# Attention and two feed-forward layers on one core: when the turns of p run, on which half of the array's rows, and in how many parts their results are used

## The chip, the cores and the metric

The kernel runs on one core of a Trainium2 chip. The metric is the device time of one execution in microseconds (us), median of several runs; lower is better. PE is TensorE (matmuls and transposes; PEld its weight loads), DVE is VectorE, ACT ScalarE, POOL GpSimd, SP SyncE, which issues DMAs. All data is float32.

## The reference

Four batches of eight heads of attention over 576 positions of 64 numbers, with rotary embedding of q and k, and behind it two feed-forward layers (512 to 2048 to 512) on all 2304 rows. Only the attention is touched by the change.

```
q_rot, k_rot = rotate(q), rotate(k)
scores = scale * q_rot @ k_rot^T                       # 576 x 576 for each head
scores = scores - max(scores, axis=-1)
attn = exp(scores)
attn = attn / (sum(attn, axis=-1) + 1e-09)
x = attn @ v                                           # then rows (B*S, H*D)
g = h - tanh(h), h = x @ w_in;      x = g @ w_out      # layer 1
g = h * sigmoid(h), h = x @ w_in;   x = g @ w_out      # layer 2
```

## The kernel before

**Tiling.** Two heads make a pair; there are 16 pairs (`NP`), handled one after the other. Head 0 of a pair lies on partitions 0 to 63, head 1 on 64 to 127, so a matmul for one head uses one half of the array's rows ("half 0", "half 1"), and the two halves can work at the same time. The 576 query rows of a head are four tiles of 128 and one remainder of 64. A pair takes five cycles, z0 to z4, which the `while` loop at the end of `attention` writes out one after the other. In z0 to z3 a cycle has two score tiles, first that of head 0 (half 0), then that of head 1 (half 1), each of two matmuls of 288 columns (e = 0, 1), each of these with two passes in the trace. In z4 the two remainders of 64 rows share one tile.

**The way of one tile.** PE computes the scores into one of two buffers in PSUM (tag `sc`; `bufs=2`), DVE takes the row maximum (L514), ACT the exponential with the row sum (L526), which frees the buffer. The result p then has to be turned: `p_turn` transposes it in blocks of 64 columns (L580), eight for each half and tile, into two PSUM tiles, whence ACT or DVE copies it to SBUF (`evac`, L554 and L556; `ON_DVE` says which copies DVE makes). After that `pv` multiplies it with v (L617), into one PSUM tile with `Q0` = 256 query columns (e = 0) or the other 320 (e = 1). The division is done last: the row sums' reciprocals (DVE L531, L532) are spread by POOL (L534) and by PE transposes (`spread`, L542), copied by ACT (L546, L549), and multiplied in by DVE (L626).

**Order.** Every engine runs its instructions in the order in which the loop writes them. In a cycle of the kernel before PE is given: the scores of both tiles; the turns of p of the cycle before (`pu`: lag one), alternating between the halves; the `full_block` (spread, remainder, the last turns, each on the whole array); and four, four, six, four or two products with v of the pair before (`PV_N`; e = 1 in z1 and z2, e = 0 in z3, z4 and the next z0). ACT first makes the two exponentials, then the copies.

**The next pair's work.** POOL applies the rotary embedding to the next pair's k and q (`rope_ops`, three operations for each of five parts: 0 and 1 are q, 2 and 3 are k, 4 the remainder of both, tiles `ar` and `br`). `rope_push` queues them in the order (2, 3, 0, 1, 4) and four are taken in each cycle. PE turns the result for one half in eight transposes (`qk_turn`, L434) in the cycles that `QK_AT` names. The conversion of the feed-forward weights (`conv`, L133 to L166) is spread over the cycles on DVE, ACT, POOL and SP.

**Start and end.** For pair 0 nothing lies ahead, and `warm` puts idle transposes in PE's way (L484). After pair 15 a few cycles finish the products with v, together with the first feed-forward work.

Of the kernel before, what the change touches and what calls it, by code (L numbers as in the profile page):

```python
# [29 lines left out]
def kernel(  # L30
# [298 lines left out]
    WARM_Z = (0, 7, 7, 5, 3, 5)  # L329
    ON_DVE = ((1, 1), (2, 1), (4, 1))  # L330
    QK_AT = ((4, 3), (4, 1), (4, 0))
# [4 lines left out]
    def attention(conv, on_rope_done, on_scores_near, on_scores_done):  # L336
# [90 lines left out]
        def qk_turn(i, w):  # L427
# [71 lines left out]
        def scores(g):  # L499
            i, n = divmod(g, NTI)  # L500
            h, j = tiles[n]
            kq = qk_t[i]
            sc = score_tile(g)
            for e in range(2):
                for w in ((h,) if h < 2 else (0, 1)):
                    r = half[w]
                    o, c, n = (slice(0, 128), REM + j * 128, 128) if h < 2 else (r, 0, REM)
                    k0 = (0 if h == 1 else REM) + e * HALF
                    PE.matmul(sc[o, e, 0:HALF], lhsT=kq[r, 1, c:c + n], rhs=kq[r, 0, k0:k0 + HALF],  # L509
                              start=True, stop=True)  # L510
# [18 lines left out]
        def recips(i):  # L529
            r = ap.tile([128, 2, NTI], F32, tag="rr", name="rr", bufs=2)  # L530
            DVE.tensor_scalar(out=r[:, 0], in0=sum_t.pop(i), scalar1=1e-9, scalar2=None, op0=ALU.add)  # L531
            DVE.reciprocal(out=r[:, 1], in_=r[:, 0])  # L532
            wide = ap.tile([128, NTI + 1, 64], F32, tag="rw", name="rw", bufs=2)
            POOL.tensor_copy(out=wide[:, 0:NTI], in_=r[:, 1].unsqueeze(2).to_broadcast([128, NTI, 64]))  # L534
            POOL.tensor_copy(out=wide[:, NTI:], in_=r[:, 1, NTI - 1:].unsqueeze(2).to_broadcast([128, 1, 64]))
            r_t[i] = wide.rearrange("p n d -> p (n d)")

        def spread(i, e, tp):
            r = r_t[i] if e else r_t.pop(i)
            for j in ((2, 3, 4) if e else (0, 1)):  # L540
                o = j * 128 - e * Q0
# [134 lines left out]
        while True:  # L676
# [13 lines left out]
            for g in gs:  # L690
                scores(g)
# [574 lines left out]
```

## Time and profile before

| | |
|---|---|
| time, median of 3 runs | 1085.2 us (1084.88 to 1085.38) |
| the profiled execution | 1085.18 us, its span on the core 1083.4 us |
| PE busy | 1071.4 us (99%) |
| DVE, ACT, POOL busy | 817.6, 650.1, 240.1 us |
| pairs 0 and 1 | 8.95 to 43.68 us |
| pairs 2 to 14 | 43.68 to 265.12 us, 17.03 us for each |
| pair 15 and the tail | 265.12 to about 298.5 us |
| feed-forward layers | to 1083.4 us |

PE is busy for almost the whole span, and in the pairs 2 to 14 for all of it; both halves of its rows count as one PE there. A row of the timeline joins instructions of one kind that follow or overlap each other: its second number is the time from the first one's start to the last one's end, and "x8" how many there are.

### The profile page before, as it was taken

How to read it: one execution, taken by the hardware profiler on the slowest of the kernel's cores; microseconds unless marked ns; L12 is line 12 of the kernel's file. 1: busy time of each engine (PE TensorE's matmuls, PEld its weight loads, DVE VectorE, ACT ScalarE, POOL GpSimd, SP SyncE). 2: the span in 40 equal slices, each digit the busy share in tenths (PEclk: the TensorE clock that was granted, in tenths of full speed). 3: DMA queues.
4: the chain of work that ended last, by engine and by line, in shares of the span. 5: the costliest groups of instructions: out<-in, count | busy, mean ns of one | idle time of the engine just before them, and what ended most of it. 6: DMA issues, size and time to landing. Idle time of an engine off the chain costs nothing.

```text
span 1083.4 us, 19054 instructions
## 1 busy us (share of the span) xinstructions
PE 1071.4 (99%) x7026; PEld 874.3 (81%) x7026; DVE 817.6 (75%) x1407; ACT 650.1 (60%) x1411; POOL 240.1 (22%) x311
## 2 busy tenths in 40 slices
PE   9999999999999999999999999999999999999998
PEld 7677767777688898888778898888888889999997
DVE  6677777777588968999999979986556357767775
ACT  5788788887777667768656657434433335334342
POOL 6878686772011100212010100310000000000000
PEclk9999999999999999999999999999999999999999
DMA  5243333322314324533745532565434213122042
GB/s 174 72 112 87 115 94 105 112 83 71 106 45 146 117 78 125 172 112 124 223 140 196 194 98 79 192 202 188 138 117 154 88 40 99 67 68 88 29 138 78
DMA packets 91277, 126.35 MB, mean 117 GB/s; under 512 B 16432, under 2 KB 57008, under 8 KB 91184
## 3 DMA queue, kind: packets, MB, share of 16 engines
q1 hardware_dynamic: 90592, 124.75, 36.4%
q8 instruction: 55, 0.90, 0.4%
q10 hardware_dynamic: 592, 0.39, 0.1%
q14 instruction: 38, 0.31, 0.1%
HBM read 88.93 MB, written 36.18 MB: 115 GB/s over the span
## 4 chain that ended last, share of the span: by engine, by line
PE 94%; issue 2%; POOL 2%; ACT 1%; DMA 1%; DVE 0%; SPq 0%; POOLq 0%; DVEq 0%
PE hp L829 35%; PE acc L906 26%; PE sc L509 9%; PE x L617 8%; PE M L990 7%; PE tpp L580 4%; PE tpq L434 1%; PE acc L1134 1%; PE tpb L542 1%; PE tpb L596 1%; DMA wf<-wd 0%; POOL bm L416 0%; ACT p L526 0%; DMA xm<-in_k_dram 0%; POOL w L251 0%
## 5 line engine op out<-in xcount | busy, mean ns | idle before, releaser
L829 PE MATMUL hp<-xh,w 128*128 128x512 f32 (+1 forms) x1280 | 388.1, 369 | 0.0
L829 PEld LDWEIGHTS hp<-xh,w 128*128 128x128 f32 x1280 | 234.5, 189 | 41.8 <-issue 1.6
L829 PE MATMUL hp<-xl,w 128*128 128x512 f32 (+1 forms) x640 | 235.9, 369 | 0.0
L840 ACT ACTIVATE t<-hp 128x512 f32<-128x512 f32 (+1 forms) x120 | 66.8, 557 | 247.3 <-PE hp L829 247.3
L906 PE MATMUL acc<-gh,w 128*128 128x512 f32 (+1 forms) x640 | 195.2, 371 | 4.0 <-ACT w L250 3.4
L874 DVE TENSOR_TENSOR gl<-t,gh 128x512 fp32r<-128x512 f32 (+1 forms) x120 | 77.5, 645 | 109.5 <-ACT gh L872 109.1
L514 DVE TENSOR_REDUCE st<-sc 128x1 f32<-128x576 f32 x144 | 103.4, 754 | 68.5 <-PE sc L509 67.3
L906 PEld LDWEIGHTS acc<-gh,w 128*128 128x128 f32 x640 | 117.8, 190 | 25.3 <-ACT w L250 3.8
L829 PEld LDWEIGHTS hp<-xl,w 128*128 128x128 f32 x640 | 120.7, 189 | 19.3
L526 ACT ACTIVATE p<-sc,st 128x576 f32<-128x576 f32 x144 | 105.4, 736 | 32.0 <-DVE st L514 32.0
L251 POOL TENSOR_TENSOR w<-wf,w 128x512 fp32r<-128x512 f32 x32 | 45.4, 1431 | 355.8 <-ACT w L250 352.3
L906 PE MATMUL acc<-gl,w 128*128 128x512 f32 (+1 forms) x320 | 118.3, 370 | 0.0
L509 PE MATMUL sc<-kq 64*128 64x288 f32 (+1 forms) x640 | 115.0, 426 | 0.8 <-ACT p L526 0.6
L509 PEld LDWEIGHTS sc<-kq 64*128 64x128 f32 (+1 forms) x640 | 68.9, 175 | 41.3 <-ACT p L526 16.1
L906 PE MATMUL acc<-w,gh 128*128 128x512 f32 x288 | 88.9, 390 | 0.0
L617 PE MATMUL x<-pt,vm 128*64 128x256 f32 (+1 forms) x512 | 79.1, 421 | 0.0
L872 ACT ACTIVATE gh<-t 128x512 fp32r<-128x512 f32 (+1 forms) x120 | 70.6, 588 | 6.2 <-PE acc L906 6.2
L990 PE MATMUL M<-w,gh 128*128 128x256 f32 x384 | 70.3, 283 | 0.0
L906 PEld LDWEIGHTS acc<-gl,w 128*128 128x128 f32 x320 | 60.8, 190 | 10.1
L580 PE MATMUL tpp<-ident,p 64*128 64x64 f32 x1248 | 68.2, 225 | 0.0
L580 PEld LDWEIGHTS tpp<-ident,p 64*128 64x128 f32 x1248 | 63.5, 138 | 4.0 <-DVE xl L811 0.4
L990 PEld LDWEIGHTS M<-w,gh 128*128 128x128 f32 x384 | 61.8, 191 | 2.3
(135 smaller groups left out, 1878.0 us busy)
## 6 DMA issues: line engine op xcount, KB each, us to landing
raw<-in_moe_w_in_dram SPq DMA_DIRECT2D x32, 512.0 KB, 4.1
raw<-in_moe_w_out_dram SPq DMA_DIRECT2D x28, 512.0 KB, 3.7
xin<-xd SPq DMA_DIRECT2D x56, 256.0 KB, 4.5
wd<-wa SPq DMA_DIRECT2D x48, 256.0 KB, 2.2
wf<-wd SPq DMA_DIRECT2D x48, 256.0 KB, 3.9
pd<-xo SPq DMA_DIRECT2D x34, 256.0 KB, 3.4
xo<-pd SPq DMA_DIRECT2D x18, 256.0 KB, 5.6
xm<-in_q_dram SPq DMA_DIRECT2D x16, 256.0 KB, 3.2
```

The source lines that it names most:

```text
L251: (DVE if key[0] == 3 else POOL).tensor_tensor(out=w[:, 1].rearrange("p (a b) -> p a b", a=a), in0=src, in1=w[:, 0].bitcast(F32).rearrange ...
L509: PE.matmul(sc[o, e, 0:HALF], lhsT=kq[r, 1, c:c + n], rhs=kq[r, 0, k0:k0 + HALF], start=True, stop=True)
L514: DVE.tensor_reduce(out=st, in_=s_t[g][:, :, 0:HALF], op=ALU.max, axis=AX.XY, negate=True)
L526: ACT.activation(out=p.rearrange("p (e s) -> p e s", e=2), in_=sc[:, :, 0:HALF], func=ACTF.Exp, bias=st, accum_out=sum_t[i][:, n:n + 1])
L580: PE.transpose(tp[w][:, x * 64:x * 64 + 64], t[r, c:c + 128], ident[r, r])
L617: PE.matmul(x[o, 0:w], lhsT=l, rhs=r, start=(cc == 0), stop=(cc == NJ))
L829: PE.matmul(hp, lhsT=w[:, a, ws], rhs=bb, start=(n == 0), stop=(n == 3 * KD - 1))
L840: ACT.activation(out=t, in_=hp, func=ACTF.Tanh, scale=0.5 if l else 1.0)
L872: ACT.activation(out=gh, in_=t, func=ACTF.Copy)
L874: DVE.tensor_tensor(out=gl, in0=t, in1=gh.bitcast(F32), op=ALU.subtract)
L906: PE.matmul(acc, lhsT=a, rhs=bb, start=(fi == 0 and n == 0), stop=(fi == NH - 1 and n == 2))
L990: PE.matmul(prod_t[name][:, tt], lhsT=al[i], rhs=bw[j], start=(first and tt == 0 and x == 0), stop=(last and tt == nt - 1 and x == 2))
```

## The change

Five things. (1) The turns of p lag two cycles instead of one: those of tile u come two cycles after its scores (z2 turns tile 0, ..., the next pair's z0 tile 3 and z1 tile 4). (2) PE is given, in z0 to z3: the first score matmul of head 0; all turns of half 1; the other three score matmuls; all turns of half 0. So half 1 turns while half 0 does its scores, and the other way round. (3) The copies of the turned p that ACT makes come ahead of its exponentials, and DVE makes five of them in each pair instead of three. (4) Reciprocals are taken and spread in two parts: the first four row sums in z2, the other five in the next pair's z0; the products with v start with e = 0, in z4, and e = 1 takes z2 and z3. So z1 has four products of 256 columns instead of 320, and z3 the reverse. (5) POOL makes the remainder's rope parts first; pair 1 turns its q on half 1 in z2 instead of z1; the idle transposes at the start are dealt out otherwise.

```diff
@@ -326,9 +326,9 @@
     NPV = 4 * (NJ + 1)
     Q0 = 256
     WARM = (5, 5, 6, 2, 4, 1, 6)
-    WARM_Z = (0, 7, 7, 5, 3, 5)
-    ON_DVE = ((1, 1), (2, 1), (4, 1))
-    QK_AT = ((4, 3), (4, 1), (4, 0))
+    WARM_Z = (0, 12, 7, 5, 2, 0)
+    ON_DVE = ((1, 0), (2, 0), (2, 1), (3, 0), (4, 0))
+    QK_AT = ((4, 3), (4, 2), (4, 0))
     R_K = 1
     PV_N = (4, 4, 6, 4, 2)
     CONV_K = (0, 1, 1, 1, 1)
@@ -428,13 +428,18 @@
             rot = rot_t[i]
             r = half[w]
             tp = ps.tile([128, 512], F32, tag="tp", name="tpq", bufs=3)
-            for t in range(2):
-                for j in range(NJ):
-                    o = (t * NJ + j) * 64
-                    PE.transpose(tp[:, o:o + 64], rot[t][r, j].rearrange("p h d -> p (h d)"), ident[r, r])
-            return lambda: ACT.activation(
+            turns = [(tp[:, n * 64:n * 64 + 64], rot[n // NJ][r, n % NJ].rearrange("p h d -> p (h d)"), r)
+                     for n in range(2 * NJ)]
+            return turns, lambda: ACT.activation(
                 out=qk_t[i][:, :, REM:S].rearrange("p t (j w c) -> p t j w c", j=NJ, w=2)[:, :, :, w],
                 in_=tp.rearrange("p (t j c) -> p t j c", t=2, j=NJ), func=ACTF.Copy)
+
+        def turn(*lists):
+            for x in range(max(len(n) for n in lists)):
+                for n in lists:
+                    if x < len(n):
+                        o, t, r = n[x]
+                        PE.transpose(o, t, ident[r, r])
 
...
-        def scores(g):
+        def scores(g, e):
...
+            for w in ((h,) if h < 2 else (0, 1)):
+                r = half[w]
+                o, c, n = (slice(0, 128), REM + j * 128, 128) if h < 2 else (r, 0, REM)
+                k0 = (0 if h == 1 else REM) + e * HALF
+                PE.matmul(sc[o, e, 0:HALF], lhsT=kq[r, 1, c:c + n], rhs=kq[r, 0, k0:k0 + HALF],
+                          start=True, stop=True)
...
-        def recips(i):
+        def recips(i, e):
+            n0, n = (4, NTI - 4) if e else (0, 4)
             r = ap.tile([128, 2, NTI], F32, tag="rr", name="rr", bufs=2)
-            DVE.tensor_scalar(out=r[:, 0], in0=sum_t.pop(i), scalar1=1e-9, scalar2=None, op0=ALU.add)
-            DVE.reciprocal(out=r[:, 1], in_=r[:, 0])
-            wide = ap.tile([128, NTI + 1, 64], F32, tag="rw", name="rw", bufs=2)
-            POOL.tensor_copy(out=wide[:, 0:NTI], in_=r[:, 1].unsqueeze(2).to_broadcast([128, NTI, 64]))
-            POOL.tensor_copy(out=wide[:, NTI:], in_=r[:, 1, NTI - 1:].unsqueeze(2).to_broadcast([128, 1, 64]))
-            r_t[i] = wide.rearrange("p n d -> p (n d)")
+            sums = (sum_t.pop(i) if e else sum_t[i])[:, n0:n0 + n]
+            DVE.tensor_scalar(out=r[:, 0, 0:n], in0=sums, scalar1=1e-9, scalar2=None, op0=ALU.add)
+            DVE.reciprocal(out=r[:, 1, 0:n], in_=r[:, 0, 0:n])
+            wide = ap.tile([128, n + e, 64], F32, tag=f"rw{e}", name="rw", bufs=1)
+            POOL.tensor_copy(out=wide[:, 0:n], in_=r[:, 1, 0:n].unsqueeze(2).to_broadcast([128, n, 64]))
+            if e:
+                POOL.tensor_copy(out=wide[:, n:], in_=r[:, 1, n - 1:n].unsqueeze(2).to_broadcast([128, 1, 64]))
+            r_t[i, e] = wide.rearrange("p n d -> p (n d)")
 
         def spread(i, e, tp):
-            r = r_t[i] if e else r_t.pop(i)
-            for j in ((2, 3, 4) if e else (0, 1)):
-                o = j * 128 - e * Q0
-                PE.transpose(tp[:, o:o + 128], r[:, j * 128:(j + 1) * 128], ident)
+            r = r_t.pop((i, e))
+            for j in range(2 + e):
+                PE.transpose(tp[:, j * 128:j * 128 + 128], r[:, j * 128:(j + 1) * 128], ident)
...
-        def p_turn(i, u):
+        def p_turn(i, u, w):
             e, o = place(u)
-            if u in (0, Q0 // 128):
+            if w and u in (0, Q0 // 128):
...
+            r = half[w]
+            tp = ps.tile([128, 512], F32, tag="tp", name="tpp", bufs=3)
...
+            (early if act else dve).append(out)
+            return [(tp[:, x * 64:x * 64 + 64], t[r, c:c + 128], r) for x, (t, c) in enumerate(src)]
...
-            e = 1 - e
...
         def rope_push(i):
-            for n in (2, 3, 0, 1, 4):
+            for n in (4, 2, 3, 0, 1):
                 rq.extend((i, f) for f in rope_ops(i, n, POOL))
...
-            for g in gs:
-                scores(g)
+            early.clear(), dve.clear(), late.clear()
+            pu = (i, z - 2) if z > 1 else (i - 1, z + NJ - 1)
+            has = 0 <= pu[0] < NP
+            if more and z == 0:
+                qk_alloc(i + 1)
+            qk = [w for w in range(2) if more and z == qk_at[w]]
+
+            def q_turn(w, outs):
+                t, f = qk_turn(i + 1, w)
+                outs.append(f)
+                return t
+
+            if len(gs) > 1:
+                scores(gs[0], 0)
+                if has:
+                    turn(p_turn(*pu, 1))
+                scores(gs[0], 1)
+                scores(gs[1], 0)
+                scores(gs[1], 1)
+                if has:
+                    turn(p_turn(*pu, 0))
+                for w in qk:
+                    turn(q_turn(w, early if i < 2 else late))
+            else:
+                for g in gs:
+                    scores(g, 0)
+                    scores(g, 1)
+                if qk:
+                    turn(p_turn(*pu, 1), q_turn(0, early))
+                    turn(p_turn(*pu, 0))
+                elif has:
+                    turn(*[p_turn(*pu, w) for w in (1, 0)])
...
+            rest, e0, e1 = live and z == 3, live and z == 3, i and z == 1
+            rem = more and z == (R_K if i else 2)
+            if rest or e1 or rem:
+                tp = ps.tile([128, 512], F32, tag="tp", name="tpb", bufs=3)
+            if rest:
+                rest_turn(i, tp[:, Q0:])
+                late.append(spread(i, 0, tp))
+            if e1:
+                late.append(spread(i - 1, 1, tp))
+            if rem:
+                rem_turn(i + 1, tp[:, 384:])
+                late.append(lambda: rem_evict(i + 1, tp[:, 384:]))
+            for f in early:
                 f()
-            if gs:
-                row_max(gs[-1])
-            for act, f in outs:
-                if not act:
-                    f()
+            for g in gs:
+                row_max(g)
+            for f in dve:
+                f()
+            if live and z == 2:
+                recips(i, 0)
             if i and z == 0:
-                recips(i - 1)
+                recips(i - 1, 1)
             if more and z == (0 if i else 1) and i + 2 < NP:
                 rope_push(i + 2)
             if live:
@@ -749,15 +758,14 @@
                 on_scores_near(z)
             for g in gs:
                 exps(g)
-            for act, f in outs:
-                if act:
-                    f()
-            if i and z == 1:
-                pvq.extend((i - 1, m) for m in range(NPV))
+            for f in late:
+                f()
+            if live and z == NJ:
+                pvq.extend((i, m) for m in range(NPV))
             conv.run(CONV_K[z] if i < NP - (z > 1) else 0)
             if i * (NJ + 1) + z < len(WARM_Z):
                 warm(WARM_Z[i * (NJ + 1) + z], idle)
-            for _ in range(PV_N[z] if live or z == 0 else NPV // 2):
+            for _ in range(PV_N[z] if i < NP or z < 2 else NPV // 2):
```

On PE, these are z1 and z2 of an early pair; `sc` are scores, `tpp` turns of p, `tpq` turns of the next pair's k and q, `tpb` the whole-array work, `x` the products with v. Before:

```order
L509 MATMUL sc<-kq 128x288 x4
L580 MATMUL tpp<-ident,p 128x64 x16
L542 MATMUL tpb<-ident,rw 128x128 x3
L440 MATMUL tpb<-ident,ar 128x128
L617 MATMUL x<-pt_766,vm 64x320 x4
L509 MATMUL sc<-kq 128x288 x4
L580 MATMUL tpp<-ident,p 128x64 x16
```

and the same place after:

```order
L513 MATMUL sc<-kq 128x288
L442 MATMUL tpp<-ident,p 128x64 x7
L513 MATMUL sc<-kq 128x288 x3
L442 MATMUL tpp<-ident,p 128x64 x7
L548 MATMUL tpb<-ident,rw 128x128 x3
L445 MATMUL tpb<-ident,ar 128x128
L619 MATMUL x<-pt_389,vm 64x256 x2
L619 MATMUL x<-pr_390,vr_170 64x256 x2
L513 MATMUL sc<-kq 128x288
L442 MATMUL tpp<-ident,p 128x64 x8
L513 MATMUL sc<-kq 128x288 x3
L442 MATMUL tpp<-ident,p 128x64 x8
```

The turns of half 1 have moved ahead of three of the four score matmuls, and z1's products have become narrower.

On POOL, this is the end of pair 1's rope and the beginning of pair 2's, during pair 0 (`rw` are the spread reciprocals). Before:

```order
L416 TENSOR_TENSOR bm<-xm_190,csq 128x256
L420 TENSOR_TENSOR aq<-aq,bm 128x4x64
L410 TENSOR_TENSOR ar<-xr,csr 128x128
L416 TENSOR_TENSOR br<-xr,csr 128x128
L420 TENSOR_TENSOR ar<-ar,br 128x128
L410 TENSOR_TENSOR ak<-xm_345,csk 128x4x64
```

and after:

```order
L416 TENSOR_TENSOR bm<-xm_190,csq 128x256
L420 TENSOR_TENSOR aq<-aq,bm 128x4x64
L410 TENSOR_TENSOR ar<-xr,csr 128x128
L416 TENSOR_TENSOR br<-xr,csr 128x128
L420 TENSOR_TENSOR ar<-ar,br 128x128
L410 TENSOR_TENSOR ak<-xm_345,csk 128x4x64
L540 COPY rw<-rr 128x256
L416 TENSOR_TENSOR bm<-xm_345,csk 128x256
```

The rows of `ar` and `br` read alike, but before they end pair 1's rope and after they begin pair 2's: pair 1's own three stand at the very start, ahead of its first `ak`. The first copy of reciprocals (pair 0's first four sums) now stands behind all of this; before, the first one came after pair 2's whole rope.

On DVE, these are the maxima of z4 and of the next pair's z0 with what lies between. Before:

```order
L514 TENSOR_REDUCE st<-sc 128x1
L151 SCALAR_TENSOR_TENSOR wa<-wm,wa 128x512
L514 TENSOR_REDUCE st<-sc 128x1 x2
L556 COPY pt_1633<-tpp 128x4x64
L556 COPY pr_1634<-tpp 64x64
L556 COPY pr_1634<-tpp 128x2x64
L531 TENSOR_SCALAR rr<-sums 128x9
L532 RECIPROCAL rr<-rr 128x9
```

and after:

```order
L518 TENSOR_REDUCE st<-sc 128x1
L562 COPY pt_1409<-tpp 128x8x64 x2
L151 SCALAR_TENSOR_TENSOR wa<-wm,wa 128x512
L518 TENSOR_REDUCE st<-sc 128x1 x2
L562 COPY pt_1409<-tpp 128x8x64
L537 TENSOR_SCALAR rr<-sums 128x5
L538 RECIPROCAL rr<-rr 128x5
```

Two copies of turned p now stand ahead of L151 and of the next pair's first maximum; the copy in three pieces moved on to z1.

## Rows read from the trace of the kernel before

**Rows 1.** The page, busy time of each engine: us, share of the span, instructions
```profile
PE 1071.4 (99%) x7026; PEld 874.3 (81%) x7026; DVE 817.6 (75%) x1407; ACT 650.1 (60%) x1411; POOL 240.1 (22%) x311
```

**Rows 2.** Busy time by stretch: start:end, length, then the columns named
```profile
core 0: us, PE busy (x) PEld busy (x) DVE busy (x) ACT busy (x) POOL busy (x), PEclk, DMA share, GB/s
8.95:43.68 34.73, 32.95 (x335) 24.38 (x335) 25.02 (x40) 24.87 (x64) 33.08 (x48) 1.00 0.37 114
43.68:265.12 221.44, 221.44 (x2368) 155.58 (x2366) 165.84 (x300) 182.45 (x482) 155.53 (x220) 1.00 0.34 97
298.50:1083.40 784.90, 776.42 (x3998) 666.20 (x3996) 600.92 (x1010) 415.03 (x801) 48.60 (x34) 1.00 0.38 122
```

**Rows 3.** The same view, sum over the five cycles of one pair, 196.99 to 214.02
```profile
sum 17.03, PE 17.03 PEld 11.96 DVE 12.86 ACT 14.04 POOL 12.69; mean PE 3.41 PEld 2.39 DVE 2.57 ACT 2.81 POOL 2.54
```

**Rows 4.** Timeline of PE in that pair: start, us, instruction, count
```profile
196.99 1.64 PE L509 MATMUL sc<-kq 64*128 64x288 f32 x8
...
200.50 1.46 PE L509 MATMUL sc<-kq 64*128 64x288 f32 x8
...
202.96 1.30 PE L617 MATMUL x<-pt,vm 128*64 128x320 f32 x8
204.19 1.27 PE L509 MATMUL sc<-kq 64*128 64x288 f32 x8
205.26 0.69 PE L580 MATMUL tpp<-ident,p 64*128 64x64 f32 x16
...
207.64 1.27 PE L509 MATMUL sc<-kq 64*128 64x288 f32 x7
208.72 0.22 PE L580 MATMUL tpp<-ident,p 64*128 64x64 f32 x1
208.76 0.40 PE L509 MATMUL sc<-kq 64*128 64x288 f32 x1
...
210.17 1.08 PE L617 MATMUL x<-pt,vm 128*64 128x256 f32 x8
211.18 1.19 PE L509 MATMUL sc<-kq 64*64 64x288 f32 x8
```

**Rows 5.** Timeline of ACT in that pair
```profile
199.84 0.73 ACT L526 ACTIVATE p<-sc,st 128x576 f32<-128x576 f32 x1
```

**Rows 6.** Timeline of DVE in that pair; in brackets the idle time before and its releaser
```profile
198.26 1.42 DVE L514 TENSOR_REDUCE st<-sc 128x1 f32<-128x576 f32 x2 [0.70 <-PE sc L509]
...
200.68 0.21 DVE L532 RECIPROCAL rr<-rr 128x9 f32<-128x9 f32 x1
...
206.87 0.68 DVE L556 COPY pt<-tpp 128x512 f32<-128x512 f32 x1
...
213.16 1.43 DVE L151 SCALAR_TENSOR_TENSOR wa<-wm,wa 128x512 f32<-128x512 f32 x1
```

**Rows 7.** Timeline of POOL in that pair
```profile
212.78 1.27 POOL L166 TENSOR_TENSOR w<-wa,w 128x512 fp32r<-128x512 f32 x1
```

**Rows 8.** All of line L151 in the span: ns min/median/max, first and last start
```profile
L151 DVE SCALAR_TENSOR_TENSOR wa<-wm,wa x64: 672/688/1816, 24.5 to 838.9; 128x512 f32<-128x512 f32 x64
```

**Rows 9.** Timeline of POOL at the start, pair 1's rope and the beginning of pair 2's
```profile
9.43 0.90 POOL L410 TENSOR_TENSOR ak<-xm,csk 128x256 f32<-128x256 f32 x1 [8.12 <-DMA xm<-in_k_dram]
...
18.37 0.45 POOL L410 TENSOR_TENSOR ar<-xr,csr 128x128 f32<-128x128 f32 x1
...
20.17 0.73 POOL L410 TENSOR_TENSOR ak<-xm,csk 128x256 f32<-128x256 f32 x1
```

**Rows 10.** Timeline of PE in pairs 0 and 1
```profile
20.20 0.40 PE L434 MATMUL tpq<-ident,ak 64*128 64x64 f32 x4
...
22.55 1.19 PE L509 MATMUL sc<-kq 64*64 64x288 f32 x8
...
32.04 0.55 PE L542 MATMUL tpb<-ident,rw 128*128 128x128 f32 x3 [0.80 <-POOL rw L534]
```

**Rows 11.** SP's issue of the remainder of k of pair 1
```profile
7.09 0.61 SPq L370 DMA_DIRECT2D xr<-in_k_dram  x1
```

**Rows 12.** Time from issue to landing of pair 1's two remainders
```profile
DMA to landing us min/median/max: 3.5/3.6/3.8
```

More of the change, by code (lines that the diff above doesn't have):

```diff
@@ L503, in scores @@
             sc = score_tile(g)
[L504 to L510, printed above, removed]
+            for w in ((h,) if h < 2 else (0, 1)):
[4 more added lines that the diff above has]
+                          start=True, stop=True)
         def row_max(g):
@@ L597, in rest_turn @@
                              p_t[i, a].rearrange("p h s -> p (h s)")[:, MAIN:MAIN + 128], ident)
-            return False, lambda: evac(pt_t[i][0][1], t, False)
+            dve.append(lambda: evac(pt_t[i][0][1], t, False))
         x_t = {}
@@ L619, in pv @@
                 x_out(i, x, rs_t.pop((i, e)), e)
-                if e == 0:
+                if e:
                     del pt_t[i], v_t[i]
@@ L631, in x_out @@
                 nc.sync.dma_start(out=xd[0][B][:, c, b * REM:(b + 1) * REM], in_=xs[:, w - REM:w])
-        pvq, rq = [], []
+        pvq, rq, early, dve, late = [], [], [], [], []
         def rope_push(i):
-            for n in (2, 3, 0, 1, 4):
+            for n in (4, 2, 3, 0, 1):
                 rq.extend((i, f) for f in rope_ops(i, n, POOL))
@@ L695, in attention @@
                 warm(WARM[6], idle)
-            if more and z == 0:
-                qk_alloc(i + 1)
-            outs, early = [], []
-            pu = (i, z - 1) if z else (i - 1, NJ)
-            def full_block():
-                if live:
-                    es = ((), (1,), (), (0,), ())[z] if i else ()
-                else:
-                    es = (1, 0) if z == 1 else ()
-                rest = live and z == 3
-                rem = more and z == (R_K if i else 3)
-                if rest or rem or es:
-                    tp = ps.tile([128, 512], F32, tag="tp", name="tpb", bufs=3)
-                if rest:
-                    outs.append(rest_turn(i, tp[:, Q0:]))
-                for e in es:
-                    outs.append((True, spread(i - 1, e, tp)))
-                    if len(es) > 1 and e:
-                        tp = ps.tile([128, 512], F32, tag="tp", name="tpb", bufs=3)
-                if rem:
-                    x = 384 if i else 0
-                    rem_turn(i + 1, tp[:, x:x + 128])
-                    outs.append((True, lambda: rem_evict(i + 1, tp[:, x:x + 128])))
@@ L722, in attention @@
-            if z >= 4:
-                full_block()
-            for w in range(2):
-                if more and z == qk_at[w]:
-                    (early if z else outs).append((True, qk_turn(i + 1, w)))
-            if pu[0] >= 0 and (live or z == 0):
-                outs.extend(p_turn(*pu))
-            if z < 4:
-                full_block()
-            if len(gs) > 1:
-                row_max(gs[0])
-            for act, f in early:
-                f()
-            if gs:
-                row_max(gs[-1])
@@ L773, in attention @@
                 on_tail()
-                if z and not pvq:
+                if z > 1:
                     break
```

23 lines of the change are left out of this document (8 added, 15 removed).

## Prediction

> **What bounds the kernel now.** I first read the page's busy times: PE 99%, no other engine over 75% [rows 1]. Then the busy times by stretch. In the pairs 2 to 14 PE is busy for all of 221.44 us, 17.03 for each pair; in the feed-forward layers for 776.42 of 784.90; only in the pairs 0 and 1 is it idle for 1.78 us [rows 2]. The granted clock reads 1.00 in all three stretches, so nothing is to be had from it. In one pair taken by itself the next engines are ACT with 14.04 and DVE with 12.86 of 17.03 [rows 3].
>
> A PE that is always busy can still lose time here, since a matmul on half of the array's rows counts as busy while the other half stands still. That is read from the timeline of PE. In z2 all eight passes of both score tiles lie within 1.27 us, from 204.19 on [rows 4]; half 0's turns of p follow 1.07 after the start, so one tile alone takes 1.07, and the two tiles run side by side. In z0 the same eight passes take 1.64, in z1 1.46, and in z3 1.52 (207.64 to the end of the pass at 208.76) [rows 4]. The excess over z2 is **0.37, 0.19 and 0.25**: the second tile started late, because its buffer is one of two and is free only when the exponential two tiles earlier has read it. In z1 this can be followed: the exponential of z0's second tile runs from 199.84 for 0.73, to 200.57 [rows 5], and the cycle had begun at 200.50. During the wait half 1 has nothing to do: its turns stand behind its own scores in program order. Then, when half 1 does its turns, half 0 is done.
>
> **The change part by part.** *The order of turns and scores.* With a lag of two cycles, half 1 has turns to do that need nothing of the cycle before, and they stand ahead of the second tile's scores. Eight turns of a half take about 0.62 (an estimate: the start at 205.26 and 0.69 for all sixteen, side by side [rows 4]). The late buffer is hidden behind them if it comes less than 0.62 after the cycle's start. Half 0 then needs 1.07 + 0.62 = 1.69, half 1 0.62 + 1.07 = 1.69: the length of z2 now. So z0, z1 and z3 lose their excess, 0.37 + 0.19 + 0.25 = 0.81.
>
> Not all of that stays, because the ring of score, maximum, exponential and buffer keeps its own pace. From the start of z0 at 196.99, the maxima begin at 198.26 and take 1.42 for two [rows 6], the second exponential follows at 199.84 and ends at 200.57 [rows 5], and the second tile of z1 starts about 0.15 later, at 200.72 (200.50 plus the excess): 3.73 after the start of z0. DVE's two maxima follow each other without a gap, so an earlier second tile in z0 does not shorten this. z0 without its excess lasts 3.50 - 0.37 = 3.13, so the second tile of z1 comes 0.60 into z1. That is just when half 1's turns end, with a load of the first weights before it; I take off 0.1. The other cycles: half 1 now changes once more, from turns to scores, which costs between nothing and 0.04 each time (z2's two tiles start within 0.2 of each other with all loads in it, 1.27 against 1.07 [rows 4]); that z4 and z2 lose small delays too is within the same size. So 0.81 - 0.1 = 0.71, with bounds of 0.55 and 0.83, and I take **0.70 for a pair**.
>
> *The products by halves.* The 256-column and 320-column products change places between z1 and z3: eight passes take 1.08 or 1.30 [rows 4], so z1 gains 0.22 and z3 loses 0.22. Sum nothing. Which cycle is shorter matters only to the ring, and z1 is the one that starts late, so nothing is gained there either.
>
> *DVE and ACT.* Two copies of 512 elements move from ACT to DVE, 0.68 each [rows 6], and the reciprocals become two pairs of small operations instead of one, which costs about 0.4 (a reciprocal is 0.21 [rows 6], the addition ahead of it no more). DVE gets 12.86 + 1.36 + 0.4 = 14.6 in 16.3 us, 90%; ACT falls to about 12.9, 79%. ACT's copies come ahead of its exponentials; they need only turns that end while the scores still run, so they lie in the time in which ACT waits for DVE's maxima. What hides the dearer DVE is the ring's slack: in z2 and z3 there is some, in z4 and z0 hardly (first rival). POOL's new copies (4 and 5 sums instead of 9) have the same elements and half a pair of time before the spread needs them: nothing.
>
> *The start.* This is the part that costs. POOL's first rope part for pair 1 is now the remainder, whose k is issued at 7.09 [rows 11] and lands 3.5 later [rows 12], so 10.6 instead of 9.43 [rows 9]. The remainder takes 20.17 - 18.37 = 1.80, the twelve others 18.37 - 9.43 = 8.94: pair 1's q is ready at 21.3 instead of 18.37, and PE's turn of it, which had come at 20.20 without a wait [rows 10], now waits for up to 1.2. Then the first reciprocals of pair 0, which the last whole-array work of z3 reads, stand behind pair 2's remainder and its first operation: 21.3 + 1.80 + 0.73 + 0.5 for the copy = 24.3. After that come the spread and some PE work, so z4 of pair 0 starts about 25.3 instead of 22.55 [rows 10], 2.75 late. Part of it comes back: the wait of 0.80 at 32.04 for the old reciprocals [rows 10] goes, since POOL is ahead there, and pair 1's cycles gain their 0.7. Left: 2.75 - 0.80 - 0.70 = **1.2 lost**, with bounds of 0.3 (the idle transposes that fill PE's waits, 27 before and 26 now, cost nothing then) and 2.75.
>
> *The end.* Pair 15 gains as the others. The feed-forward layers are bound by PE with 776.42 of 784.90 [rows 2], have the same instructions and simply start earlier; nothing, within 1.
>
> **Sum.** 13 pairs of rows 2 and pair 15: 14 x 0.70 = 9.8; less 1.2: 8.6. The profiled execution took 1085.18, as the median 1085.2: **1076.6 us**.
>
> **Rivals.** *DVE is late in z4* (same side, less). There one maximum, two copies (1.36) and L151 stand ahead of the next pair's first maximum. The scores of z4 take 1.19, the maximum about 0.71 (half of 1.42), so the copies end about 3.3 after the start of z4, which lasts 2.8; the maximum of z0 may begin at 2.8 + 1.27 = 4.1. L151 fits with its median of 0.69 [rows 8], but in this pair it took 1.43 [rows 6], while POOL's L166 ran from 212.78 for 1.27 [rows 7]. If POOL still overlaps it, the maximum is 0.3 to 0.6 late and the ring passes that on to z1. At 0.4 late a pair gains 0.3: 14 x 0.3 - 1.2 = 3.0, **1082.2**. For it: POOL has the same work in a shorter pair. Against: the copies push L151 back, behind the end of L166.
>
> *PE keeps strict order across the halves* (slower). Then the eight turns of half 1 start only after both passes of the first score matmul, the next passes only after the last turn, and half 0's turns only after the last pass of the second tile. With about 0.24 between passes (1.07 for four, less the first load) and 0.06 between turns: passes at 0.1 and 0.35, turns to 0.8, six passes to 2.0 at least, eight turns to 2.5, minus overlaps about 2.25, against 1.69 forecast: 0.55 in each of four cycles, 2.2 a pair. 14 x (2.2 - 0.70) + 1.2 = 22, **1107**. The point from which it decides is whether an instruction of one half may start before an older one of the other. The trace says that it may: z2's second tile, behind all passes of the first, does not wait for them (1.27 for both), and a turn starts at 208.72, before the last score pass at 208.76 [rows 4]. The Trainium skill, page "TensorE: Matmul & The Clock Gate", section "Part 3: Packing small matmuls — row/col tiling", speaks for this rival: it says that matmuls start and end strictly in program order, and that only weight loads for other rows are pulled ahead. The row at 208.72 disagrees with that for its start, and the measurement decides.
>
> *The change does not bring the halves together* (no gain). If switching a half between turns and scores costs what the excess gave, some 0.2 in each of four cycles, the pairs stay at 17.03 and the start remains: **1086.4**.
>
> *More comes back.* The start costs only 0.3, a pair gains 0.83, and the feed-forward part gains a little: 14 x 0.83 - 0.3 = 11.3, with up to 1 more: **about 1073**.
>
> **How the numbers follow.** Forecast 0.65; DVE late 0.20; strict order 0.04; no gain 0.07; more 0.04. A measurement tells 0.2% (2.2 us) from no change, so faster means under 1083.0: the forecast, the last rival and most of the first (0.14), 0.83; the rest of the first and the no-gain case, 0.12, is the same; slower is strict order and an expensive start, 0.05. The range leaves out the strict order and no-gain cases: from 1072.5 to 1084.
>
> **What would show it.** Right: the cycles of the middle pairs add up to about 16.3; the first row of turns lies within the score rows, which are near 1.7 long for half 1's late scores; no wait of PE at the scores except 0.1 in z1. Start: POOL's first operation at 10.6, PE waiting near 20 for q and near 22 for the reciprocals, pair 2 starting at 44.9. Wrong: DVE's maxima in z0 begin more than 1.3 after the scores with no idle time before them (first rival); gaps between turns and scores on one half (third); a start that costs over 3.

## The result and the profile after

The changed kernel takes 1076.62 us (median of 4, 1074.67 to 1077.51) against 1085.29 before (1084.88 to 1085.74): a ratio of 0.992, interval 0.990 to 0.9935. Forecast were 1076.6. The sum came out to the tenth; two of its terms did not, and they cancelled. The experiments below say which.

The profiled execution took 1074.67, at the low end. The page's busy times [rows 1]:

```profile
PE 1060.5 (99%) x7025; PEld 864.9 (81%) x7025; DVE 841.9 (78%) x1471; ACT 638.7 (60%) x1379; POOL 243.3 (23%) x327
```

Busy time by stretch of the same profile: the pairs 0 and 1, the pairs 2 to 14, the feed-forward layers, as [rows 2]; then the five cycles z0 to z4 of one middle pair and their sum, as [rows 3]. The columns are start:end, length, then PE, PEld, DVE, ACT, POOL, granted clock, DMA share and GB/s.

```profile
9.55:44.12 34.57, 32.21 (x332) 23.11 (x331) 27.23 (x46) 24.24 (x62) 32.99 (x50) 1.00 0.38 114
44.12:256.91 212.79, 212.65 (x2369) 148.29 (x2367) 185.38 (x352) 173.01 (x456) 157.56 (x233) 1.00 0.34 100
288.00:1072.90 784.90, 776.89 (x4002) 666.12 (x3998) 600.89 (x1010) 415.35 (x802) 49.58 (x34) 1.00 0.38 122
...
207.88:211.06 3.18, 3.18 (x42) 2.52 (x40) 3.18 (x5) 1.98 (x6) 0.87 (x1) 1.00 0.83 223
211.06:214.43 3.37, 3.37 (x36) 2.38 (x34) 2.50 (x8) 3.03 (x9) 2.69 (x7) 1.00 0.15 48
214.43:217.87 3.44, 3.44 (x38) 2.30 (x37) 3.28 (x8) 3.37 (x12) 3.06 (x5) 1.00 0.28 68
217.87:221.38 3.51, 3.51 (x39) 2.47 (x37) 2.46 (x5) 3.49 (x9) 3.43 (x6) 1.00 0.46 146
221.38:224.22 2.84, 2.84 (x38) 1.74 (x36) 2.84 (x6) 1.44 (x5) 2.76 (x4) 1.00 0.14 46
sum 16.34, PE 16.34 PEld 11.41 DVE 14.26 ACT 13.31 POOL 12.81; mean PE 3.27 PEld 2.28 DVE 2.85 ACT 2.66 POOL 2.56
```

PE is still busy for all of a middle pair, but the pair is 16.34 long and not 17.03. DVE is now busy for all of z4 and z0 (2.84 of 2.84, 3.18 of 3.18): the place that the first rival named.

How the halves share a cycle is seen in PE's timeline, here z0 and the beginning of z1 [rows 4]:

```profile
207.88 0.51 PE L513 MATMUL sc<-kq 64*128 64x288 f32 x1
207.89 0.52 PE L442 MATMUL tpp<-ident,p 64*128 64x64 f32 x5
208.23 0.40 PE L513 MATMUL sc<-kq 64*128 64x288 f32 x1
208.25 0.35 PE L442 MATMUL tpp<-ident,p 64*128 64x64 f32 x3
208.44 0.70 PE L513 MATMUL sc<-kq 64*128 64x288 f32 x4
208.96 0.22 PE L442 MATMUL tpp<-ident,p 64*128 64x64 f32 x1
208.98 0.40 PE L513 MATMUL sc<-kq 64*128 64x288 f32 x1
...
210.05 1.08 PE L619 MATMUL x<-pt,vm 128*64 128x256 f32 x8
211.06 0.51 PE L513 MATMUL sc<-kq 64*128 64x288 f32 x1
211.07 0.52 PE L442 MATMUL tpp<-ident,p 64*128 64x64 f32 x5
```

The first score pass of half 0 and the first turn of half 1 start within 0.01 of each other, and the eight turns lie between and beside the passes. Half 0's first turn starts at 208.96, 1.08 after the cycle's start (1.07 in z2 before), while half 1 is still at its scores (208.98).

### The profile page after: what moved, and what is told of

It is laid out like the page before. It is cut to its first block, busy times and chain, and to the rows that moved or that the text cites. A ratio compares the mean times of both kernels' runs of the same rounds, so it can differ in the third digit from the quotient of the medians.

```text
span 1072.9 us, 19128 instructions
## 1 busy us (share of the span) xinstructions
PE 1060.5 (99%) x7025; PEld 864.9 (81%) x7025; DVE 841.9 (78%) x1471; ACT 638.7 (60%) x1379; POOL 243.3 (23%) x327
## 4 chain that ended last, share of the span: by engine, by line
PE 93%; issue 2%; POOL 2%; DMA 1%; DVE 0%; ACT 0%; SPq 0%; POOLq 0%; ACTq 0%; DVEq 0%
PE hp L837 36%; PE acc L914 26%; PE x L619 8%; PE M L998 7%; PE sc L513 7%; PE tpp L442 5%; PE tpb L548 1%; PE acc L1142 1%; PE tpq L442 1%; PE tpb L599 1%; POOL bm L416 1%; DMA wf<-wd 0%; DMA csr<-rope_rem_dram 0%; POOL ak L410 0%; POOL aq L410 0%
## 5 line engine op out<-in xcount | busy, mean ns | idle before, releaser
L513 PE MATMUL sc<-kq 64*128 64x288 f32 (+1 forms) x640 | 132.6, 423 | 2.1 <-ACT p L530 1.9
L513 PEld LDWEIGHTS sc<-kq 64*128 64x128 f32 (+1 forms) x640 | 80.5, 176 | 40.0 <-ACT p L530 21.9
L442 PE MATMUL tpp<-ident,p 64*128 64x64 f32 x1248 | 102.8, 225 | 0.0
L442 PEld LDWEIGHTS tpp<-ident,p 64*128 64x128 f32 x1248 | 91.6, 139 | 10.0 <-issue 7.3
L619 PE MATMUL x<-pt,vm 128*64 128x320 f32 (+1 forms) x512 | 79.5, 421 | 0.1
```

The lines of the kernel that those rows point to most:

```text
L442: PE.transpose(o, t, ident[r, r])
L619: PE.matmul(x[o, 0:w], lhsT=l, rhs=r, start=(cc == 0), stop=(cc == NJ))
```

## Where the time went

Two profiles of the changed kernel, the one above and one more of the same code (the first experiment), cut at the same instructions. Each number is the distance between the starts of two matmuls; the first row begins and the last row ends with the span. The fifth row ends with the 41st feed-forward matmul.

| stretch | before | after | after, again |
|---|---|---|---|
| up to the first scores | 8.95 | 9.55 | 9.33 |
| pairs 0 and 1 | 34.73 | 34.57 | 37.21 |
| pairs 2 to 14 | 221.44 | 212.79 | 212.23 |
| pair 15 up to its z4 | 14.08 | 13.62 | 13.60 |
| z4 of pair 15 and the tail | 20.30 | 19.11 | 19.10 |
| the rest of the feed-forward layers | 783.90 | 783.26 | 783.83 |
| span | 1083.4 | 1072.9 | 1075.3 |

The pairs save what they were to save: 9.1 and 9.7 with pair 15, against a forecast of 9.8. The pairs 0 and 1 differ by 2.6 between two executions of one kernel. And the tail saves 1.2, for which the prediction had nothing.

## The experiments

For the pairs 2 to 14 the table gives their whole length and a thirteenth of it; it depends little on the start. The times are medians, with the median of before from the same chip and the ratio's interval.

| run | pairs 2 to 14 | a pair | time | before | ratio, interval |
|---|---|---|---|---|---|
| the change, again | 212.23 | 16.33 | 1077.08 | 1085.82 | 0.991 to 0.994 |
| scores first | 222.28 | 17.10 | 1089.23 | 1085.82 | 1.002 to 1.004 |
| before, new order | 227.65 | 17.51 | 1093.62 | 1085.82 | 1.006 to 1.009 |
| three copies on DVE | 220.45 | 16.96 | 1085.32 | 1085.82 | 0.998 to 1.0005 |
| one more on DVE | 219.48 | 16.88 | 1084.86 | 1085.33 | 0.999 to 1.0006 |
| z4's copy on ACT | 212.44 | 16.34 | 1077.87 | 1085.33 | 0.992 to 0.995 |
| rope queued later | 212.59 | 16.35 | 1076.56 | 1085.33 | 0.991 to 0.994 |
| both of these | 212.62 | 16.36 | 1076.02 | 1085.33 | 0.990 to 0.993 |
| k first | 212.69 | 16.36 | 1074.77 | 1085.82 | 0.988 to 0.991 |
| k first, L151 in z0 | 211.74 | 16.29 | 1074.22 | 1085.82 | 0.988 to 0.991 |

**The same kernel again.** No edit.

> The changed kernel once more, unaltered, for a second profile of it. If the saving is made of the middle pairs, each takes 16.34 us again (17.03 before) and the time is 1076.6 within 1.5. If the first profile, 1.9 us below the median, was short because of the feed-forward part or the first scores, this one differs from it there and not in the pairs.

Measured: 1077.08 (1075.87 to 1079.17), 16.33 a pair. This profile is 2.4 longer than the first. The feed-forward part gives 0.6 of it, as guessed; the pairs 0 and 1, which the expectation had not named, give 2.6, and the other stretches are together 0.8 shorter. What happens in the pairs 0 and 1 comes with the last experiments.

**PE's order undone, and with it the place of ACT's copies**, which go back behind the exponentials.

```diff
-            (early if act else dve).append(out)
+            (late if act else dve).append(out)
...
-                scores(gs[0], 0)
+                for g in gs:
+                    scores(g, 0)
+                    scores(g, 1)
                 if has:
-                    turn(p_turn(*pu, 1))
-                scores(gs[0], 1)
-                scores(gs[1], 0)
-                scores(gs[1], 1)
-                if has:
-                    turn(p_turn(*pu, 0))
+                    turn(*[p_turn(*pu, w) for w in (1, 0)])
```

> The lag of two cycles, the products by halves, the reciprocals in two parts and the five copies on DVE stay; only PE's order in z0 to z3 goes back: the scores of both tiles first, then the turns of both halves side by side, with ACT's copies behind its exponentials as they were. Theory (the order hides the late buffer): the second tile waits with an idle half again, some 0.25 to 0.4 in z0, z1 and z3, a pair takes about 17.0, the time is 1086. Rival (the gain comes from the products by halves or from the copies on DVE): 16.4 a pair, 1076.6.

17.10 a pair, 1089.23. PE's timeline in z2 of a pair:

```profile
209.33 1.42 PE L513 MATMUL sc<-kq 64*128 64x288 f32 x7
210.56 0.27 PE L442 MATMUL tpp<-ident,p 64*128 64x64 f32 x1
210.59 0.40 PE L513 MATMUL sc<-kq 64*128 64x288 f32 x1
210.67 0.81 PE L442 MATMUL tpp<-ident,p 64*128 64x64 f32 x15
```

The scores end at 210.99, 1.66 after their start instead of the 1.27 of z2 before, and half 1 has nothing to do until its own begin. So the lag, the products by halves, the split reciprocals and the two more copies on DVE give nothing in the pairs by themselves (17.10 against 17.03): the saving goes with the order. ACT's copies were moved back in the same run. That they lengthen the pair is not what the trace shows: the exponentials of z2 begin 2.13 after its start here and 2.37 in the changed kernel, so ACT is not later. The 3 us beyond the expected 1086 are 0.1 in each pair and the start, less 1.3 in the tail: pair 2 begins at 48.52 here, 4.8 later than before.

**PE's order alone done**, in the kernel before, with its lag of one cycle: `scores` and the turns are cut as in the change, and z0 to z3 read

```diff
+            if len(gs) > 1:
+                scores(gs[0], 0)
+                if pt:
+                    pt[0](1)
+                scores(gs[0], 1)
+                scores(gs[1], 0)
+                scores(gs[1], 1)
+                if pt:
+                    pt[0](0)
...
```

> The kernel before with only PE's new order in z0 to z3 (first score matmul, turns of half 1, the other score matmuls, turns of half 0) and the old lag of one cycle. Theory: the turns of half 1 then need the same exponential that frees the second tile's buffer, so half 1 waits as long as before and nothing is gained: 17.0 a pair, 1085 within 1.5. Rival (the order alone does it): about 16.4 a pair, 1077.

Both expectations missed: 17.51 a pair, 1093.62, slower than before by 0.6 to 0.9%. PE's timeline in z2:

```profile
210.29 0.75 PE L508 MATMUL sc<-kq 64*128 64x288 f32 x2
210.84 0.52 PE L581 MATMUL tpp<-ident,p 64*128 64x64 f32 x5
211.15 0.51 PE L508 MATMUL sc<-kq 64*128 64x288 f32 x1
...
211.39 0.70 PE L508 MATMUL sc<-kq 64*128 64x288 f32 x3
```

The turns of half 1 begin 0.55 after the cycle's start. ACT's timeline before them, and from the list of waits between 100 and 200 that of PE's weight loads for these turns (in total, how often, the longest):

```profile
209.48 0.73 ACT L525 ACTIVATE p<-sc,st 128x576 f32<-128x576 f32 x1
210.20 0.59 ACT L553 ACTIVATE pt<-tpp 128x512 f32<-128x512 f32 x1
...
PEld tpp L581 <- ACT pt L553: 1.6, 6, 0.3
```

The theory is not what holds z2: the exponential that these turns need ended at 210.21, before the cycle began (210.29). They start 0.05 after the end of a copy (210.20 for 0.59) that empties one of the three PSUM tiles which all turns share (tag `tp`), and that ACT makes behind its exponentials in the kernel before. In z1 it is the same with a copy of DVE; in z0, and for 0.1 in z3, the turns do wait for the exponential. By cycles, against before: z0 3.50 (3.51), z1 3.84 (3.69), z2 3.99 (3.45), z3 3.34 (3.54). So the two cycles in which the theory holds lose nothing, and the two that wait for an empty tile lose 0.69.

And while the turns of half 1 wait, half 0 stands still as well: the pass at 211.15 is that of its own second score matmul, which stands behind the turns in program order. It comes 0.86 after the start, where 0.35 and another 0.24 would be its own pace, and the second tile's scores only follow from 211.39 on; before, all eight passes took 1.27 in z2 [rows 4]. So the order alone costs 0.48 a pair, and the lag without the order gains nothing. Whether the order needs the lag, or ACT's copies ahead of the exponentials so that a PSUM tile is empty, or both, no run tells.

**Three copies on DVE instead of five.**

```diff
-    ON_DVE = ((1, 0), (2, 0), (2, 1), (3, 0), (4, 0))
+    ON_DVE = ((1, 0), (2, 0), (4, 0))
```

> The changed kernel with three copies on DVE instead of five: of z4 one and of z0 the one go back to ACT, ahead of its exponentials. Theory (the ring through z0's maxima and exponentials sets z1): z0's maxima come 0.07 earlier, but ACT's copy of half 0 ends only about 2.3 us into z0, where its exponential now starts at 2.18, so the second tile of z1 is 0.05 to 0.15 later and a pair takes 16.4 to 16.5: 1077 to 1079. Rival (DVE, full in z4 and z0, holds the pair): 16.27, 1075.6.

Far worse than expected: 16.96 a pair, and nearly all of the saving in the pairs is gone (1085.32 in time). ACT's timeline of this run, in z0 of one pair (which began at 199.92) and in z4 (from 213.81):

```profile
202.00 0.60 ACT L560 ACTIVATE pt<-tpp 128x512 f32<-128x512 f32 x1 [0.64 <-PE sc L513]
202.50 0.74 ACT L530 ACTIVATE p<-sc,st 128x576 f32<-128x576 f32 x1
...
215.74 0.60 ACT L560 ACTIVATE pt<-tpp 128x512 f32<-128x512 f32 x1 [1.39 <-PE tpq L442]
216.23 0.59 ACT L433 ACTIVATE kq<-tpq 128x512 f32<-128x512 f32 x1
```

In z0 the copy of half 0's turns, which come last in the cycle, stands ahead of the exponentials: the first begins at 2.58 after the start of z0, where it begins at 2.18 in the changed kernel, and z0 takes 3.46 instead of 3.18. In z4 the copy stands ahead of that of the next pair's q (L433), which the next pair's first scores need: they begin at 216.88, and z4 takes 3.07 instead of 2.84; z1 is 0.12 longer too. What looked like a load put on DVE for nothing is worth 0.6 in each pair.

**One more operation on DVE in z4**, which nothing else reads.

```diff
+        junk = ap.tile([128, 512], F32, name="junk")
...
+            if live and z == NJ and 1 < i < NP - 1:
+                DVE.tensor_tensor(out=junk, in0=junk, in1=junk, op=ALU.mult)
```

> The changed kernel with one more DVE operation of 512 elements (about 0.65 us, on a tile that nothing else reads) in z4 of the pairs 2 to 14, behind the two copies. Theory (DVE has no slack left between z4 and z0's maxima, and the ring passes what is late there to the second tile of z1): z0's maxima begin 0.65 later, z1's second tile comes at about 1.2 instead of 0.60, and a pair takes 16.9: 13 times 0.55 more, 1083.8. Rival (z1 is set by PE's own rows, and DVE catches up in z0): 16.34 a pair, 1076.6.

16.93 for each pair that follows one with the operation, 1084.86. DVE's timeline from z4 into the next z0 (which begins at 214.70):

```profile
213.91 1.27 DVE L563 COPY pt<-tpp 128x512 f32<-128x512 f32 x2
215.11 0.99 DVE L749 TENSOR_TENSOR junk<-junk 128x512 f32<-128x512 f32 x1
216.03 0.68 DVE L151 SCALAR_TENSOR_TENSOR wa<-wm,wa 128x512 f32<-128x512 f32 x1
216.63 1.41 DVE L519 TENSOR_REDUCE st<-sc 128x1 f32<-128x576 f32 x2
```

The maxima begin 1.94 into z0 instead of 1.34, 0.60 later, and the pair is 0.59 longer: one for one. DVE has no slack there. Only the place differs from the expectation: 0.48 of it is in z0's own length, since the first tile of z1 waits too, and 0.12 in z1.

**One copy of z4 back on ACT, behind the exponential.**

```diff
-    ON_DVE = ((1, 0), (2, 0), (2, 1), (3, 0), (4, 0))
+    ON_DVE = ((1, 0), (2, 1), (3, 0), (4, 0))
...
-            (early if act else dve).append(out)
+            (late if (u, w) == (2, 0) else early if act else dve).append(out)
```

> The changed kernel with one of the two copies in z4 back on ACT, behind z4's exponential, where ACT is idle. Theory (DVE is late by the little that z4 puts on it): z0's maxima begin at 1.27 after the scores and not at 1.34, z1's second tile at 0.56 and not at 0.60, and a pair takes 16.27: 1075.7. Rival (the second tile is bound by half 1's turns): 16.34.

No gain: 16.34. DVE had 0.60 less to do, and this is what became of it (DVE, then POOL, in z4 and the next z0):

```profile
209.22 0.68 DVE L562 COPY pt<-tpp 128x512 f32<-128x512 f32 x1
209.81 1.59 DVE L151 SCALAR_TENSOR_TENSOR wa<-wm,wa 128x512 f32<-128x512 f32 x1
211.33 1.41 DVE L518 TENSOR_REDUCE st<-sc 128x1 f32<-128x576 f32 x2
...
209.59 1.26 POOL L166 TENSOR_TENSOR w<-wa,w 128x512 fp32r<-128x512 f32 x1
```

L151 starts 0.60 earlier and now meets POOL's L166 for 1.04 instead of 0.44: it takes 1.59, where it took 0.98 in the changed kernel and has a median of 0.69 [rows 8]. The maxima begin when they began before, with DVE busy up to them: the time that the copy left free went into an overlap that it had kept short. There was little to gain in any case, as the last run shows.

**Pair 2's rope queued one cycle later.**

```diff
-            if more and z == (0 if i else 1) and i + 2 < NP:
+            if more and z == (0 if i else 2) and i + 2 < NP:
```

> The changed kernel with pair 2's rope queued one cycle later, so that pair 0's first reciprocals no longer stand behind four of its operations on POOL. Theory: the copy of the reciprocals ends about 20.4 instead of 22.9, the wait of 0.81 of PE at 22.92 goes, and pair 2 starts 0.8 earlier: 1075.8. Rival (the wait only moves to the next cycle that needs POOL, pair 1's z2): no change of pair 2's start.

No change that can be told: 1076.56. The wait at the spread of pair 0 is gone, but PE waits elsewhere at the start (PE's timeline; in brackets the idle time and its releaser):

```profile
22.35 0.46 PE L442 MATMUL tpq<-ident,aq 64*128 64x64 f32 x4 [1.23 <-POOL aq L420]
...
33.92 0.55 PE L548 MATMUL tpb<-ident,rw 128*128 128x128 f32 x3 [1.39 <-POOL rw L540]
```

The wait moved, as the rival had it. This is no clean test of the theory, since POOL as a whole is late in this profile, its first operation coming at 11.56. With the copy of z4 on ACT as well:

> The two edits together: one copy of z4 on ACT, and pair 2's rope queued one cycle later. If both theories hold they add: 16.27 a pair and pair 2 0.8 earlier, 1074.9.

1076.02 and 16.36 a pair: neither theory held by itself, and their sum does not either.

**Pair 1's k first.** The remainder's rope goes behind k for pair 1, together with the later queueing.

```diff
-            for n in (4, 2, 3, 0, 1):
+            for n in (4, 2, 3, 0, 1) if i > 1 else (2, 3, 4, 0, 1):
```

> The changed kernel with pair 1's rope in the order k, remainder, q (the remainder no longer first), and pair 2's rope queued one cycle later. Theory (the start waits for POOL, whose rope stands still until the remainder's k has landed, between 9.7 and 11.7 in the profiles): POOL starts at about 9.4 in every execution, q of pair 1 is ready at about 20, no wait of PE at the turn of q nor at the first spread, no stretch at half clock behind them, and pair 2 starts at 44.2 or earlier: 1074.6, with less spread from run to run. Rival (the start is late for another reason, as the first scores): pair 2 at 45.5 to 46.5, 1076.6.

1074.77, and all its runs lie between 1074.55 and 1075.01, where those of the changed kernel spread over 2.8 and 3.3 us. With the later queueing alone it was 1076.56. Pair 2 begins at 43.48; the pairs 0 and 1 take 34.75 here, against 34.57 and 37.21. The start in three profiles; first the changed kernel's first profile (POOL, then PE), where the remainder's k landed early:

```profile
9.73 0.45 POOL L410 TENSOR_TENSOR ar<-xr,csr 128x128 f32<-128x128 f32 x1 [8.43 <-DMA xr<-in_k_dram]
...
22.92 0.44 PE L548 MATMUL tpb<-ident,rw 128*128 128x128 f32 x2 [0.81 <-POOL rw L540]
23.19 0.71 PE L489 MATMUL x<-ident 128*128 128x128 f32 x5
```

then its second profile, with the stretches behind the wait (third column from the end: the granted clock):

```profile
10.87 0.45 POOL L410 TENSOR_TENSOR ar<-xr,csr 128x128 f32<-128x128 f32 x1 [9.57 <-DMA xr<-in_k_dram]
...
23.92 0.51 PE L548 MATMUL tpb<-ident,rw 128*128 128x128 f32 x2 [1.56 <-POOL rw L540]
24.23 1.27 PE L489 MATMUL x<-ident 128*128 128x128 f32 x5
25.43 2.19 PE L513 MATMUL sc<-kq 64*64 64x288 f32 x8
...
24.20:25.40 1.20, 1.20 (x7) 0.90 (x5) 0.93 (x2) 0.38 (x1) 1.12 (x3) 0.50 0.00 0
25.43:27.60 2.17, 2.17 (x11) 0.81 (x10) 0.48 (x1) 0.00 (x0) 2.09 (x3) 0.51 0.18 28
```

and the kernel with k first:

```profile
9.13 0.98 POOL L410 TENSOR_TENSOR ak<-xm,csk 128x256 f32<-128x256 f32 x1 [7.82 <-DMA xm<-in_k_dram]
...
19.92 0.39 POOL L540 COPY rw<-rr 128x256 f32<-128x256 f32 x1
...
31.61 0.55 PE L548 MATMUL tpb<-ident,rw 128*128 128x128 f32 x3 [0.97 <-POOL rw L540]
```

In the changed kernel POOL's first operation for pair 1 hangs on a small transfer that lands at another time in each execution: it begins between 9.73 and 11.73 in the eight profiles of kernels with its order. When it is late, PE waits 1.56 for the first spread instead of 0.81, and behind that wait the granted clock reads 0.50 (1.2 GHz) until 27.6, so that z4's scores take 2.19 instead of 1.19. With k first there is no wait at the turn of q nor at the first spread, and the clock stays at 1.00 there.

**L151 moved away from L166**, in addition: `CONV_K` becomes (1, 1, 1, 1, 0), with no step in the very first cycle, so that L151 comes behind the maxima of the next z0.

> As the run before, and the fourth step of the weights' conversion (L151) moves from z4 to the next pair's z0, behind its maxima, where it does not meet POOL's L166 and DVE has 0.8 us idle. Theory (the ring through z0's maxima costs the last 0.05 in z1): z0's maxima begin at 1.27, z1's second tile comes at 0.56 instead of 0.60, a pair takes 16.27: 14 times 0.06 less, 1073.8. Rival (half 1's turns set z1): 16.33 a pair, 1074.6.

16.29 a pair, 1074.22 (1073.67 to 1074.67): the fastest of all, 0.9 to 1.2% faster than before, though between it and the run before there is only half a microsecond. DVE's timeline in z0 (from 190.48):

```profile
191.82 1.42 DVE L518 TENSOR_REDUCE st<-sc 128x1 f32<-128x576 f32 x2 [0.92 <-PE sc L513]
...
194.06 0.65 DVE L151 SCALAR_TENSOR_TENSOR wa<-wm,wa 128x512 f32<-128x512 f32 x1
```

DVE now waits 0.92 for the scores, L151 takes 0.65, the exponentials begin 0.05 earlier, and so does the second tile of z1 (0.56 instead of 0.60), as the theory had it. But the maxima begin at 1.34 all the same, now with DVE idle before them. So the 0.07 that I had laid to DVE's being late is not that, and it is no work of the new order either, for in z2 of the kernel before (from 204.19) the maxima begin 1.34 after the start too:

```profile
205.53 1.42 DVE L514 TENSOR_REDUCE st<-sc 128x1 f32<-128x576 f32 x2 [2.01 <-PE sc L509]
```

What makes it 1.34 in some cycles and 1.27 in others is open.

## Why the prediction was right, step by step

**A pair gains 0.70: right, and for the reason given.** In this pair 0.69 was measured, over the pairs 2 to 14 of the two profiles 0.67 and 0.71. By cycles, [rows 4] against the five stretches above: z0 from 3.51 to 3.18 (forecast 0.37 less), z1 from 3.69 to 3.37 (0.19 + 0.22 less, and the ring's 0.1 more), z2 from 3.45 to 3.44, z3 from 3.54 to 3.51 (0.25 less and 0.22 more), z4 unchanged. The second tile of z1 starts 0.60 after the cycle's start, as forecast; that this was met so exactly is luck, since z0 took 3.18 and not 3.13, and the ring from z0's start to that tile 3.78 and not 3.73. (The 3.73 rests on that tile's own start at 200.72, 0.22 into z1, and not on 200.50 plus the excess of 0.19, as the prediction has it.) The scores-first run shows the converse: take the order away and the saving in the pairs is gone.

**The first rival was there, at an eighth of its size.** The maxima of z0 begin at 1.34 after the start with DVE busy up to them, the sign that the prediction gave for it. The sign was a weak one, since they begin at 1.34 with DVE idle as well. L151 took 0.98 and not 1.43, because the two copies pushed it to the end of L166, which was the argument against. With L151 moved away a pair takes 16.29: the rival cost about 0.05 of the 0.4 assumed. That the place is tight was right: 0.60 more of DVE work there costs 0.59.

**ACT's and DVE's copies: priced from one side only.** The prediction counted what DVE gets, and ACT's copies as hidden. Both hold for the kernel as it is (DVE is busy for 14.26 in a pair, forecast 14.6; ACT for 13.31, forecast 12.9). What it did not see is why five copies must be on DVE: two of them on ACT, ahead of what the next step waits for, cost 0.6 a pair.

**PE across the halves: right, with a limit that the prediction did not see.** Had the turns and scores started in program order, a pair would have been 1.5 longer than before, by the prediction's estimate. The Trainium skill, page "TensorE: Matmul & The Clock Gate", section "Part 3: Packing small matmuls — row/col tiling", says that matmuls start strictly in program order. The timeline above disagrees for the starts: half 0's first turn (208.96) starts ahead of the last score matmul of half 1 (208.98), which stands before it in program order, and five turns start between the two passes of the first score matmul (207.88 and 208.23). The limit is a wait: in the kernel before with the new order, half 0's second score matmul did not start ahead of half 1's older turns while these waited (211.15, 0.27 later than its own pace). In the changed kernel the turns have what they need when the cycle begins, and so they hold up nothing.

**The start: mechanism right, size wrong, by an amount that changes with the execution.** Forecast: POOL begins at 10.6, the first spread waits, 1.2 lost by pair 2's start. The first profile loses 0.44 by the start of pair 2, with POOL beginning at 9.73 and a remainder that takes 1.36 instead of 1.80; it is 0.60 late at the first scores already, and the pairs 0 and 1 make up 0.16. The second loses 2.86, of which 0.38 before the first scores, with POOL at 10.87: the wait is 0.75 longer, and the half clock behind it takes 1.6 more (1.27 instead of 0.71 for five idle transposes, 1.0 in z4), which no row of the kernel before had shown. Most executions seem to be of the second kind: k first makes the time 1.85 to 2.3 less than the medians of the changed kernel, and the spread goes with it.

**The tail: a term left out.** Priced at nothing, it saves 1.2. The products with v begin in the pair's own z4 now and no longer in the next pair's z1, so fewer are left at the end. In this stretch PE's timeline counts 52 passes of products before and 40 after; twelve take about 1.5 (eight start within 1.01 in z0 above). Two spreads fewer and the wait ahead of them are 0.4 less, sixteen turns more are 0.65 more (0.62 for sixteen side by side): 1.25 together. This is read from the two traces and was not tested alone, but two runs bear it out: with the lag and the products of the change and the scores first, this stretch takes 18.98; with PE's new order alone in the kernel before, 20.29.

So 1076.6 was hit by luck: a saving of 1.2 was left out at the end, and a loss of some 1 to 1.7 (an estimate from the second profile and the medians) at the start. The range would have held without that luck; the tenth would not.

## What to carry to other kernels

An engine that is 99% busy may be two half engines that wait for each other: compare the length of the same pair of operations in several places, and the longer ones tell what the shorter ones cost. Work that fills such a hole must have all that it needs when the hole opens, its operands and an empty tile to write to; if it waits itself, it holds up the other half's work that stands behind it. And a first operation that hangs on the last small transfer makes the time of the whole program vary: put ahead of it whatever has its data.

## What the runs showed of the hardware

**The clock.** In five profiles PE waited 1.39 to 1.56 us for the first spread, and in all five a stretch with a granted clock of 0.50 (1.2 GHz) began, once during the wait and four times 0.2 to 1.1 behind it, though PE had idle transposes and scores to do behind the wait; in the one shown it covers 24.2 to 27.6. Behind the wait of 0.81 the clock stayed at 1.00, and so it did in the run with the rope queued later, behind 1.23 at 22.35 and 1.39 at 33.92, and in the run with both edits, behind 1.51 at 33.54. What tells these apart is open.

**DVE beside POOL.** L151, which reads two tiles of SBUF, takes 0.65 where it does not meet POOL's L166 (the run with L151 moved away) and has a median of 0.69 [rows 8], 0.98 when L166 ends 0.44 after its start, and 1.59 when L166 ends 1.04 after its start: it loses most of the time of the overlap, while L166 takes 1.26 or 1.27 each time. The Trainium skill, page "SBUF — State Buffer", section "SBUF: two separate sides", calls the port that the two engines share a lock that one instruction holds to its end, while the other is blocked; these rows agree.
